# Stores and weight loads in other slots, and two blocks' exponentials taken from PSUM, in a kernel of chunk attention and two feed-forward layers

## Chip, cores and metric

The kernel runs on one core of a Trainium2 chip. The metric is the time of one execution in microseconds (us) on the device, lower is better. The engines are named as the profile names them: PE (TensorE, matmul), PEld (its weight loads), DVE (VectorE), ACT (ScalarE), POOL (GpSimd) and SP (SyncE), whose queue issues every DMA of this kernel.

## What is computed

Attention within chunks of 64 positions, then a gated layer, then a layer with a clipped quadratic activation, each followed by a projection:

```python
# q, k, v: (8 batches, 8 heads, 576 positions, 64), chunks of 64
scores = scale * matmul(q_c, k_c^T); scores -= max(scores)
attn = exp(scores); attn /= sum(attn) + 1e-9
x = matmul(attn, v_c)            # as (4608 tokens, 512)
gate = 1 / (1 + exp(-(x @ w_gate))); val = x @ w_val      # (512, 1536) each
y = (gate * val) @ w_out         # (1536, 512)
h = y @ w_in                     # (512, 2048)
g = where(h >= 1, h, where(h <= -1, 0, (h + 1)**2 / 4))
out = g @ w_out2                 # (2048, 512)
```

The inputs are fp32, except that the weights arrive as 64-bit numbers whose two words the kernel puts together itself ("rounding" below).

## The kernel before

**Blocks and slots.** The 4608 tokens are handled in 9 blocks of 512. The first stage, up to 743.8 us, is a loop over the blocks `b` and over the 12 groups `f` of 128 gate and value columns. Each `(b, f)` has two slots, numbered `24 * b + 2 * f` for the gate projection and one more for the value projection: 216 slots. A projection is 12 matmuls of 128x512 on PE (`pr`, L476 to L478). After the gate projection ACT takes the sigmoid into a tile `sg` (L880, four such tiles in turn), after the value projection DVE multiplies into it (L883), and SP stores it to `gT` in DRAM (`g_store`, L766).

**What lies between the projections.** Everything else of the stage is hung on slots by a table, `at(slot, prio, fn, args)`, and `emit(slot)` writes out what is due, ordered by the slot's fraction, then by `prio`, then by when it was entered. Every engine works its instructions off in the order in which they are written. So the table sets the order on each queue; it sets no time.

**Attention.** The attention of block `b` is spread over slots of block `b - 1`, as four head pairs `p`. Per pair: loads of q and k (`load`, 8 or 16 DMAs, L282) and of v (`v_load`, 4 or 6 DMAs, L297); `t`, transposes on DVE (`qkT`, L307); `s`, the scores on PE into two PSUM banks (`S`, L324); `m`, row maxima on DVE and their subtraction into the SBUF tile `sp` (L334, L338); `e`, the exponential on ACT in place (L344); `n`, the row sums and reciprocals on DVE (L349 to L352); `w`, the multiplication by the reciprocals on POOL (L357); `p`, a transpose on PE (`PT`, L363); `c`, its copy by ACT (L366); `o`, the product with v on PE (`O`, L377); `x` and `l`, the high part by ACT and the low part by DVE (L393, L397), which the projections of the next block read. From block 2 on a pair begins every 6 slots, with `s` in its slot 2, `p` in 6, `c` in 7 and `o` in 8. Block 1 begins a pair every 5 slots. Block 0 has nothing to hide behind: `first_block` writes its four pairs out by hand ahead of the first projection, by the string `ORDER`, where `s` stands for `s`, `m`, `e` in a row, `n` for `n`, `w`, `p` for `p`, `c` and `o` for `o`, `x`, `l`.

**Rounding of weights.** In slots 26 to 186 the weights of the later layers are prepared, one pair of row blocks every 7 slots (`s_prep`): two loads of 512 KB into tiles `raw` (`w_load`, L103 or L107), from 4 slots later on DVE `w_low` (L112), `w_bits` (L118) and `w_join` (L129), ACT `w_scale` (L125), POOL sums (L151 to L154), then four pieces `st` on ACT and POOL (`s_split`, L173 and L174) that SP stores again (`s_spool`, L183). `raw` and `st` share a ring of `pool["nraw"]` tiles, 8 of them.

The later stages (from 743.8 us: three further products) are not touched by the change.

Of the kernel before, what the change touches and what calls it, by code (L numbers as in the profile page):

```python
# [8 lines left out]
F32 = mybir.dt.float32  # L9
# [4 lines left out]
AF = mybir.ActivationFunctionType  # L14
ALU = mybir.AluOpType
AX = mybir.AxisListType
# [13 lines left out]
def kernel(  # L30
# [15 lines left out]
    nc = tc.nc  # L46
    P = 128
# [5 lines left out]
    CH = 64  # L53
    BS = 512
    scale = 1.0 / float(D) ** 0.5
    NB = NT // BS
# [10 lines left out]
    cp = ctx.enter_context(tc.tile_pool(name="cp", bufs=1))  # L67
# [6 lines left out]

    NWT = {"o": 7 * F1 // 4, "i": 7 * F2 // 4, "p": 7 * F2 // 4}
    sw = {kind: dp.tile([n, P, 2, 2, 256], F32, name=f"sw{kind}") for kind, n in NWT.items()}

    def f32(t):
# [118 lines left out]
    def s_prep(kind, k):  # L197

        half_ = (F1 if kind == "o" else F2) // 2
        a, b = (kind, k), (kind, k + half_)  # L200
        return [
            (0, w_load, a), (0, w_load, b), (4, w_low, a), (4, w_bits, a), (5, w_scale, a), (5, w_low, b),
            (5, w_bits, b), (6, w_scale, b), (6, w_join, a), (7, w_join, b), (8, s_sums, kind, k),
            (9, s_split, kind, k, 0), (9, s_split, kind, k, 1), (10, s_split, kind, k, 2),
            (11, s_spool, kind, k, 0), (11, s_spool, kind, k, 1), (11, s_split, kind, k, 3),
            (12, s_spool, kind, k, 2), (13, s_spool, kind, k, 3),
        ]


# [2 lines left out]
    pool = {}  # L212
    X = {}

    def open_pool(key, name, side=None):
        ctx_ = ExitStack()
        pool[key] = ctx_.enter_context(tc.tile_pool(name=name, bufs=1, side=side, reuse_waits="tile"))
        pool[key + "_ctx"] = ctx_

    def close_pool(key):  # L220
        pool[key + "_ctx"].close()
# [12 lines left out]
    NC = BS // P  # L234
# [3 lines left out]
    class Whole:  # L238
# [15 lines left out]
        def load(self, p):  # L254
# [10 lines left out]
            for i, src in enumerate((q, k)):  # L265
                for off, m, bb, s0 in runs(self.b * BS, BS):
                    rows = src[bb, 2 * p:2 * p + 2, s0:s0 + m]
                    part = slice(off // NC, (off + m) // NC)
                    if how == "M":
                        nc.sync.dma_start(  # L270
                            out=t[part, i].rearrange("i h j d -> i h (j d)"),
                            in_=rows.rearrange("h (i j) d -> i h (j d)", j=NC),
                        )
                    elif how == "T":
                        for h in range(2):
                            nc.sync.dma_start(
                                out=t[part, i, :, h], in_=rows[h].rearrange("(i j) d -> i j d", j=NC)
                            )
                    else:
                        for g in range(4):  # L280
                            h, j = divmod(g, 2)
                            nc.sync.dma_start(  # L282
                                out=t[32 * g:32 * g + 32, i, off // 32:(off + m) // 32],
                                in_=rows[h, :, 32 * j:32 * j + 32].rearrange("(t i) r -> i t r", i=32),
                            )
            self.qk[p] = t

        def v_load(self, p):

            self.V[p] = t = self.alloc("vd").rearrange("p i (c e) -> p (i c) e", e=D)  # L290
            half_ = BS // 2
            for off, m, bb, s0 in runs(self.b * BS, BS):
                for swap in range(2):
                    lo, hi = max(off, swap * half_), min(off + m, (swap + 1) * half_)
                    for h in range(2):
                        if lo < hi:
                            nc.sync.dma_start(  # L297
                                out=t[heads[h ^ swap], lo // CH:hi // CH],
                                in_=v[bb, 2 * p + h, s0 + lo - off:s0 + hi - off].rearrange("(c k) d -> k c d", k=CH),
                            )  # L300
# [26 lines left out]
            self.B["s", p] = banks  # L327

        def m(self, p):
            s = self.SP[p][:, 0].rearrange("p (g h k) -> p g h k", h=2, k=CH)  # L330
            m = cp.tile([P, 2, NC], F32, tag="m0", name="m", bufs=2)
            banks = self.B.pop(("s", p))
            for h, b in enumerate(banks):
                nc.vector.tensor_reduce(out=m[:, h], in_=b, axis=AX.X, op=ALU.max)  # L334
            for h, b in enumerate(banks):
                for swap in range(2):
                    gs = slice(swap * NC // 2, (swap + 1) * NC // 2)
                    nc.vector.tensor_tensor(  # L338
                        out=s[:, gs, h ^ swap], in0=b[:, gs],
                        in1=m[:, h, gs].unsqueeze(2).to_broadcast([P, NC // 2, CH]), op=ALU.subtract,  # L340
                    )

        def e(self, p):
            nc.scalar.activation(self.SP[p][:, 0], self.SP[p][:, 0], AF.Exp, scale=scale)  # L344

        def n(self, p):
            s = self.SP[p][:, 0].rearrange("p (g k) -> p g k", k=CH)
            l = cp.tile([P, 2 * NC], F32, tag="l0", name="l", bufs=2)
            nc.vector.tensor_reduce(out=l, in_=s, axis=AX.X, op=ALU.add)  # L349
            nc.vector.tensor_scalar_add(l, l, 1e-9)  # L350
            self.B["r", p] = r = cp.tile([P, 2 * NC], F32, tag="r0", name="r", bufs=2)
            nc.vector.reciprocal(out=r, in_=l)  # L352
# [127 lines left out]
    def proj(key, b, tag):  # L480
        w = W[key]
        o = ps.tile([P, BS], F32, tag=tag, name="pr")
        kts = [slice(kt * P, (kt + 1) * P) for kt in range(KT)]
        three(o, [(w[:, 0, ks], w[:, 1, ks], X[b, kt][:, 0], X[b, kt][:, 1]) for kt, ks in enumerate(kts)])
        return o
# [61 lines left out]
    def run_step(t):  # L547
        for _, _, fn, args in sorted(sched.pop(t, []), key=lambda e: e[:2]):
            fn(*args)
# [203 lines left out]
    NS = 2 * F1  # L753
# [3 lines left out]
    def at(slot, prio, fn, *args):  # L757
        order[0] += 1
        ev.setdefault(int(slot // 1), []).append((slot % 1, prio, order[0], fn, args))

    def emit(slot):
        for _, _, _, fn, args in sorted(ev.pop(slot, []), key=lambda e: e[:3]):
            fn(*args)
# [20 lines left out]
    slot = 26  # L784
    for kind, n in (("o", F1 // 2), ("i", F2 // 2), ("p", F2 // 2)):
        for pair in range(n):
            for dt, fn, *args in s_prep(kind, pair):
                at(slot + dt, 6 + dt / 10, fn, *args)
            slot += 7
    base = NS * (NB - 1)  # L790
    at(base, 8, close_pool, "u")
# [9 lines left out]
    for i in range(FIRST):  # L801
        key, name = ("o", 0, i), ("o", 0, 1, i)
# [52 lines left out]
    with tc.manual_schedule():  # L855
        half = cp.tile([P, 1], F32, name="half")
        nc.vector.memset(half, 0.5)
        minus = cp.tile([P, 1], F32, name="minus")
        nc.vector.memset(minus, -0.5)

        open_pool("pad", "pad", "right")
        pool["pad"].tile([P, 24], F32, name="pad")

        open_pool("pad4", "pad4", "right")
        pool["pad4"].tile([P, 704], F32, name="pad4")
        open_pool("x", "xp", "right")
        open_pool("sg", "sg", "right")
        open_pool("raw", "raw", "right")
        pool["nraw"] = 8
        open_pool("u", "au")  # L870
        first_block()
        for t in range(-6, 0):
            emit(t)
        for b in range(NB):
            for f in range(F1):
                slot = NS * b + 2 * f
                emit(slot)
                go = proj(("g", f), b, f"b{f % 2}")
                sg = pool["sg"].tile([P, BS], F32, tag="sg", name="sg", bufs=4)
                nc.scalar.activation(sg, go, AF.Sigmoid)  # L880
                emit(slot + 1)
                vo = proj(("v", f), b, f"b{2 + f % 2}")
                nc.vector.tensor_tensor(out=sg, in0=vo, in1=sg, op=ALU.mult)  # L883
                at(slot + 2, 7, g_store, b, f, sg)
        emit(NS * NB)
        close_pool("sg")
        assert not ev, ev
        open_pool("r", "rb", "right")
        for t, (fn, *args) in enumerate(steps):
            run_step(t)  # L890
            fn(*args)
        for t in sorted(sched):
            run_step(t)
        for key in ("r", "zb", "pad", "za", "y"):
            close_pool(key)
# [30 lines left out]
```

## Time and profile before

| | |
|---|---|
| median of 3 runs | 1726.3 us (1725.25 to 1729.65) |
| profiled execution | 1722.68 us, of which the span from first to last instruction is 1720.9 |
| PE busy | 1654.2 us, 96% of the span |
| DVE, ACT, POOL busy | 69%, 51%, 48% |
| DMA engines | 57.6% of 16 engines' span, 1505 issues, all on SP's queue |
| mean granted clock of TensorE | 0.984 |

The profiled execution is 3.6 us below the median of the runs; sums below are made against its span and carried over to the median as a difference. A timeline row reads: start, length, engine, line, operation, out<-in and count, and in brackets how long the engine was idle before it and who ended that. For SP a row is the time in which the queue issues the DMAs named, waits between them included; how long the data takes is a matter of other rows.

### The profile page before, as it was taken

To read this page: it belongs to the slowest core of one execution; us is meant where nothing else is said; L and a number is where in the kernel's file an instruction comes from. 1 tells how busy PE (TensorE), PEld (TensorE's weight loads), DVE (VectorE), ACT (ScalarE), POOL (GpSimd) and SP (SyncE) were. 2 spreads that over 40 slices of the span, in tenths; PEclk is the share of its full clock that TensorE was granted. 3 is DMA by queue.
4 is the path that set the end of the run, shared out by engine and by line. 5 is a ranking of instruction groups with operands and counts; after the bars stand their busy time and mean duration, and the time that the engine had idled before them with its cause. 6 is when DMAs were issued, how large, how long until landed. Compare 5 with 4: busy or idle time off the path is not lost.

```text
span 1720.9 us, 30155 instructions
## 1 busy us (share of the span) xinstructions
PE 1654.2 (96%) x10658; PEld 1518.5 (88%) x10658; DVE 1191.2 (69%) x1874; ACT 870.3 (51%) x1632; POOL 834.5 (48%) x755
## 2 busy tenths in 40 slices
PE   5889998998998999999999999999999999999998
PEld 4668886886876888899999999999999999999998
DVE  5875555564554562178777768887887879788877
ACT  4654444554544553145555555555554455545453
POOL 1431433443333442057777754534441476777675
PEclk7989999999999999999999999999999999999999
DMA  7664677776776785824554654233327954463552
GB/s 190 169 161 111 193 220 209 195 211 186 218 211 188 211 269 175 334 95 155 209 166 143 236 207 181 111 141 142 151 109 264 356 194 116 120 182 107 125 139 38
DMA packets 389671, 307.16 MB, mean 178 GB/s; under 512 B 271888, under 2 KB 302608, under 8 KB 389520
## 3 DMA queue, kind: packets, MB, share of 16 engines
q1 hardware_dynamic: 389520, 305.23, 57.6%
q8 instruction: 84, 1.38, 0.3%
q14 instruction: 67, 0.55, 0.1%
HBM read 179.83 MB, written 125.30 MB: 177 GB/s over the span
## 4 chain that ended last, share of the span: by engine, by line
PE 75%; SPq 8%; DVE 6%; DMA 6%; issue 2%; POOL 2%; ACT 1%; DVEq 0%; POOLq 0%; ACTq 0%
PE P L477 17%; PE P L478 17%; PE P L476 17%; PE pr L476 8%; PE pr L477 7%; PE pr L478 7%; SPq L282 5%; DVE z L509 2%; SPq L297 2%; DMA gT<-sg 1%; DMA raw<-in_moe_w_gate_dram 1%; PE O L377 1%; DVE z L520 1%; PE S L324 1%; DMA raw<-in_moe_w_in_dram 1%
## 5 line engine op out<-in xcount | busy, mean ns | idle before, releaser
L520 POOL TENSOR_TENSOR z<-z 128x384 fp32r<-128x384 f32 x305 | 356.4, 1191 | 308.1 <-ACT z L513 305.9
L477 PE MATMUL P<-z,w 128*128 128x384 f32 x1344 | 450.6, 335 | 5.1 <-POOL z L520 3.1
L476 PE MATMUL P<-z,w 128*128 128x384 f32 x1344 | 449.5, 334 | 0.2 <-DVE R L537 0.2
L478 PE MATMUL P<-z,w 128*128 128x384 f32 x1344 | 449.1, 334 | 0.0
L476 PE MATMUL pr<-x,w 128*128 128x512 f32 x864 | 349.0, 404 | 0.0
L477 PE MATMUL pr<-x,w 128*128 128x512 f32 x864 | 341.4, 395 | 0.3 <-DVE x L397 0.3
L478 PE MATMUL pr<-x,w 128*128 128x512 f32 x864 | 341.4, 395 | 0.0
L513 ACT ACTIVATE z<-z 128x384 fp32r<-128x384 f32 x420 | 205.8, 521 | 181.3 <-DVE z L509 106.9
L520 POOL TENSOR_TENSOR op<-in,op 128x384 fp32r<-128x384 f32 x168 | 190.6, 1153 | 148.0 <-ACT op L513 147.1
L477 PEld LDWEIGHTS P<-z,w 128*128 128x128 f32 x1344 | 252.3, 188 | 9.2 <-POOL z L520 6.6
L476 PEld LDWEIGHTS P<-z,w 128*128 128x128 f32 x1344 | 252.3, 188 | 1.1 <-DVE R L537 0.5
L478 PEld LDWEIGHTS P<-z,w 128*128 128x128 f32 x1344 | 252.3, 188 | 0.0
L883 DVE TENSOR_TENSOR sg<-pr,sg 128x512 f32<-128x512 f32 x108 | 74.5, 690 | 221.1 <-PE pr L478 118.1
L478 PEld LDWEIGHTS pr<-x,w 128*128 128x128 f32 x864 | 165.0, 191 | 35.9
L476 PEld LDWEIGHTS pr<-x,w 128*128 128x128 f32 x864 | 165.3, 191 | 35.4
L477 PEld LDWEIGHTS pr<-x,w 128*128 128x128 f32 x864 | 165.4, 191 | 33.5 <-DVE x L397 0.7
L513 ACT ACTIVATE op<-in 128x384 fp32r<-128x384 f32 x252 | 128.5, 523 | 112.8 <-PE P L478 60.1
L880 ACT ACTIVATE sg<-pr 128x512 f32<-128x512 f32 x108 | 64.5, 597 | 221.8 <-PE pr L478 212.0
L509 DVE TENSOR_TENSOR z<-z 128x384 f32<-128x384 f32 x200 | 172.4, 912 | 1.0 <-POOL z L520 0.9
L477 PE MATMUL P<-op,w 128*128 128x384 f32 x504 | 168.5, 334 | 0.1
L478 PE MATMUL P<-op,w 128*128 128x384 f32 x504 | 168.4, 334 | 0.0
L476 PE MATMUL P<-op,w 128*128 128x384 f32 x504 | 168.4, 334 | 0.0
(63 smaller groups left out, 2241.3 us busy)
## 6 DMA issues: line engine op xcount, KB each, us to landing
uT<-ua SPq DMA_DIRECT2D x96, 384.0 KB, 2.4
z<-uT SPq DMA_DIRECT2D x96, 384.0 KB, 4.1
gT<-sg SPq DMA_DIRECT2D x108, 256.0 KB, 4.4
in<-gT SPq DMA_DIRECT2D x72, 256.0 KB, 3.7
raw<-in_moe_w_out_dram SPq DMA_DIRECT2D x28, 512.0 KB, 6.2
w<-swi SPq DMA_DIRECT2D x28, 512.0 KB, 5.6
w<-swp SPq DMA_DIRECT2D x28, 512.0 KB, 6.8
swi<-st SPq DMA_DIRECT2D x24, 512.0 KB, 4.1
```

The costliest lines, as they stand in the source:

```text
L282: nc.sync.dma_start(out=t[32 * g:32 * g + 32, i, off // 32:(off + m) // 32], in_=rows[h, :, 32 * j:32 * j + 32].rearrange("(t i) r -> i t ...
L297: nc.sync.dma_start(out=t[heads[h ^ swap], lo // CH:hi // CH], in_=v[bb, 2 * p + h, s0 + lo - off:s0 + hi - off].rearrange("(c k) d -> k c ...
L324: nc.tensor.matmul(banks[h][heads[c % 2], c // 2], lhsT=t[hs, 0, ts], rhs=t[hs, 1, ts], start=True, stop=True)
L377: nc.tensor.matmul(banks[r][heads[r ^ swap], g_, i], lhsT=self.V[p][rows, c], rhs=self.SP[p][rows, 1, chunks[c]], start=True, stop=True,)
L476: nc.tensor.matmul(o, lhsT=ah, rhs=bh, start=first, stop=False, skip_group_check=open_)
L477: nc.tensor.matmul(o, lhsT=ah, rhs=bl, start=False, stop=False, skip_group_check=open_)
L478: nc.tensor.matmul(o, lhsT=al, rhs=bh, start=False, stop=last, skip_group_check=open_)
L509: (eng or nc.vector).tensor_tensor(out=op_src(p, key), in0=x, in1=y, op=ALU.subtract)
L513: nc.scalar.activation(o[:, 0], op_src(p, key), AF.Copy)
L520: eng.tensor_tensor(out=o[:, 1], in0=op_src(p, key), in1=f32(o[:, 0]), op=ALU.subtract)
L880: nc.scalar.activation(sg, go, AF.Sigmoid)
L883: nc.vector.tensor_tensor(out=sg, in0=vo, in1=sg, op=ALU.mult)
```

## The change

`s_prep` gives every step but the two loads one slot more, and the call enters the table one slot earlier. So the steps stay in the slots they had, and the two `w_load`s of each pair move one slot ahead. The priorities, `6 + dt / 10`, grow by 0.1 for the steps that have one slot more. `g_store` goes from 2 slots behind its projection's to 4. The ring of `raw` and `st` has 10 tiles for 8. For blocks 0 and 1 the scores stay in PSUM: `m_scaled` takes the maxima and multiplies them by `-scale`, and `e_sums` takes 8 exponentials of 128x64 from PSUM with the maximum as bias and the row sum as a second output, so that the subtraction and the row-sum reduction of DVE fall away.

```diff
-            (0, w_load, a), (0, w_load, b), (4, w_low, a), (4, w_bits, a), (5, w_scale, a), (5, w_low, b),
-            (5, w_bits, b), (6, w_scale, b), (6, w_join, a), (7, w_join, b), (8, s_sums, kind, k),
...
+            (0, w_load, a), (0, w_load, b), (5, w_low, a), (5, w_bits, a), (6, w_scale, a), (6, w_low, b),
+            (6, w_bits, b), (7, w_scale, b), (7, w_join, a), (8, w_join, b), (9, s_sums, kind, k),
...
+        def m_scaled(self, p):
+            m = cp.tile([P, 2, NC], F32, tag="m1", name="m", bufs=2)
+            for h, b in enumerate(self.B["s", p]):
+                nc.vector.tensor_reduce(out=m[:, h], in_=b, axis=AX.X, op=ALU.max)
+            nc.vector.tensor_scalar_mul(m, m, -scale)
+            self.B["m", p] = m
+
+        def e_sums(self, p):
...
+            for h, b in enumerate(self.B.pop(("s", p))):
+                for g in range(NC):
+                    r = h ^ (g >= NC // 2)
+                    nc.scalar.activation(
+                        s[:, g, r], b[:, g], AF.Exp, bias=m[:, h, g:g + 1], scale=scale,
+                        accum_out=l[:, g, r:r + 1],
+                    )
+
         def e(self, p):
+            if self.b < 2:
+                return self.e_sums(p)
             nc.scalar.activation(self.SP[p][:, 0], self.SP[p][:, 0], AF.Exp, scale=scale)
...
-                at(slot + dt, 6 + dt / 10, fn, *args)
+                at(slot - 1 + dt, 6 + dt / 10, fn, *args)
...
-        pool["nraw"] = 8
+        pool["nraw"] = 10
...
-                at(slot + 2, 7, g_store, b, f, sg)
-        emit(NS * NB)
+                at(slot + 4, 7, g_store, b, f, sg)
+        for t in range(3):
+            emit(NS * NB + t)
```

PE's order is the same before and after. Three places show what moves on other queues.

ACT in block 0, from pair 2's exponential on (`qkT` is pair 3's, the first `x` pair 0's). Before:

```order
L344 ACTIVATE sp<-sp 128x512
L316 ACTIVATE qkT<-T 128x4x128 x2
L393 ACTIVATE x<-O 64x256 x4
L366 ACTIVATE sp<-PT 128x512
L344 ACTIVATE sp<-sp 128x512
L393 ACTIVATE x<-O 64x256 x4
L366 ACTIVATE sp<-PT 128x512
```

After:

```order
L360 ACTIVATE sp,l<-S,m 128x64 x8
L316 ACTIVATE qkT<-T 128x4x128 x2
L420 ACTIVATE x<-O 64x256 x4
L393 ACTIVATE sp<-PT 128x512
L360 ACTIVATE sp,l<-S,m 128x64 x8
L420 ACTIVATE x<-O 64x256 x4
L393 ACTIVATE sp<-PT 128x512
```

Nothing changes places; one exponential has become eight, with the sums `l` as a second output.

DVE at the same place, from pair 2's maxima to pair 1's low part. Before:

```order
L334 TENSOR_REDUCE m<-S 128x4 x2
L338 TENSOR_TENSOR sp<-S,m 128x2x64 x4
L349 TENSOR_REDUCE l<-sp 128x8
L350 TENSOR_SCALAR l<-l 128x8
L352 RECIPROCAL r<-l 128x8
L397 TENSOR_TENSOR x<-O,x 64x256 x4
L334 TENSOR_REDUCE m<-S 128x4 x2
L338 TENSOR_TENSOR sp<-S,m 128x2x64 x4
L397 TENSOR_TENSOR x<-O,x 64x256 x4
```

After:

```order
L348 TENSOR_REDUCE m<-S 128x4 x2
L349 TENSOR_SCALAR m<-m 128x8
L377 TENSOR_SCALAR l<-l 128x8
L379 RECIPROCAL r<-l 128x8
L424 TENSOR_TENSOR x<-O,x 64x256 x4
L348 TENSOR_REDUCE m<-S 128x4 x2
L349 TENSOR_SCALAR m<-m 128x8
L424 TENSOR_TENSOR x<-O,x 64x256 x4
```

Per pair four subtractions and one reduction are gone and a small multiplication has come.

SP around slot 60 (block 4's first q and k, block 3's last v, the weights of the sixth pair). Before:

```order
L183 DMA swo<-st 128x2x512 x3
L282 DMA qk<-in_q_dram 32x8x32 x8
L282 DMA qk<-in_k_dram 32x8x32 x8
L766 DMA gT_68<-sg 128x512
L183 DMA swo<-st 128x512
L297 DMA vd<-in_v_dram 64x3x64 x2
L297 DMA vd<-in_v_dram 64x64 x2
L297 DMA vd<-in_v_dram 64x4x64 x2
L107 DMA raw<-in_moe_w_out_dram 128x512 x2
L766 DMA gT_68<-sg 128x512 x2
```

After:

```order
L183 DMA swo<-st 128x2x512 x3
L282 DMA qk<-in_q_dram 32x8x32 x8
L282 DMA qk<-in_k_dram 32x8x32 x8
L107 DMA raw<-in_moe_w_out_dram 128x512 x2
L793 DMA gT_68<-sg 128x512
L183 DMA swo<-st 128x512
L297 DMA vd<-in_v_dram 64x3x64 x2
L297 DMA vd<-in_v_dram 64x64 x2
L297 DMA vd<-in_v_dram 64x4x64 x2
L793 DMA gT_68<-sg 128x512 x2
```

The weight loads stand ahead of a store, a spool and six loads of v; the store in each place is that of the product one older than before.

## Rows read from the trace of the kernel before

**Rows 1.** Two stretches: length, busy time of the five engines, granted clock, DMA share, GB/s.

```profile
41.30:130.00 88.70, 74.95 (x529) 58.17 (x526) 72.37 (x137) 54.01 (x86) 34.91 (x26) 0.91 0.62 162
...
254.00:580.00 326.00, 302.80 (x2312) 245.38 (x2305) 176.54 (x375) 155.48 (x260) 123.73 (x128) 0.97 0.71 204
```

**Rows 2.** Timeline of PE: the product steps `O` of slots 56, 62 and 68.

```profile
235.57 0.69 PE L377 MATMUL O<-sp,vd 64*64 64x64 f32 x32
...
253.71 0.69 PE L377 MATMUL O<-sp,vd 64*64 64x64 f32 x32
...
277.94 1.13 PE L377 MATMUL O<-sp,vd 64*64 64x64 f32 x32 [4.98 <-ACT sp L366]
```

**Rows 3.** Timeline of SP's queue: stores of slots 20 to 24 and 26 to 30.

```profile
132.69 7.49 SPq L766 DMA_DIRECT2D gT<-sg  x3
...
154.03 4.28 SPq L766 DMA_DIRECT2D gT<-sg  x3
```

**Rows 4.** What SP waited for from 41 to 640 us (total, times, longest), first row.

```profile
SPq L766 <- DVE sg L883: 20.3, 13, 5.9
```

**Rows 5.** Timeline of SP's queue from 265 to 278 us.

```profile
265.70 0.40 SPq L766 DMA_DIRECT2D gT<-sg  x1
...
266.67 3.89 SPq L297 DMA_DIRECT2D vd<-in_v_dram  x6
270.90 0.81 SPq L107 DMA_DIRECT2D raw<-in_moe_w_out_dram  x2
...
272.75 2.09 SPq L183 DMA_DIRECT2D swo<-st  x2
276.96 0.33 SPq L766 DMA_DIRECT2D gT<-sg  x1
```

**Rows 6.** Timeline of DVE at 275 us: the first conversion of those weights.

```profile
275.06 0.43 DVE L112 TENSOR_SCALAR raw<-raw 128x512 int32<-128x512 uint32 x1 [9.48 <-DMA raw<-in_moe_w_out_dram]
```

**Rows 7.** Timeline of ACT: a sigmoid and the copy behind it; a later sigmoid.

```profile
251.09 0.60 ACT L880 ACTIVATE sg<-pr 128x512 f32<-128x512 f32 x1 [1.77 <-PE pr L478]
251.59 0.59 ACT L366 ACTIVATE sp<-PT 128x512 f32<-128x512 f32 x1
...
507.73 0.60 ACT L880 ACTIVATE sg<-pr 128x512 f32<-128x512 f32 x1 [2.21 <-PE pr L478]
```

**Rows 8.** SP's issue of the store that frees the tile of that later sigmoid.

```profile
504.59 0.37 SPq L766 DMA_DIRECT2D gT<-sg  x1
```

**Rows 9.** DMA issues from 500 to 510 us: count, size, median us to landing.

```profile
gT<-sg SPq DMA_DIRECT2D x2, 256.0 KB, 2.4
```

**Rows 10.** Timeline of ACT in block 0: exponentials of pairs 2 and 3.

```profile
24.52 0.63 ACT L344 ACTIVATE sp<-sp 128x512 f32<-128x512 f32 x1 [2.15 <-DVE sp L338]
...
31.43 0.63 ACT L344 ACTIVATE sp<-sp 128x512 f32<-128x512 f32 x1 [2.67 <-DVE sp L338]
31.97 1.29 ACT L393 ACTIVATE x<-O 64x256 fp32r<-64x256 f32 x4
```

**Rows 11.** Timeline of DVE: pair 2 of block 0; last, pair 0 of block 1.

```profile
22.99 0.70 DVE L334 TENSOR_REDUCE m<-S 128x4 f32<-128x256 f32 x2
23.61 0.87 DVE L338 TENSOR_TENSOR sp<-S,m 128x128 f32<-128x128 f32 x4
25.18 0.69 DVE L349 TENSOR_REDUCE l<-sp 128x8 f32<-128x512 f32 x1 [0.69 <-ACT sp L344]
25.90 0.17 DVE L350 TENSOR_SCALAR l<-l 128x8 f32<-128x8 f32 x1
...
76.55 1.53 DVE L397 TENSOR_TENSOR x<-O,x 64x256 fp32r<-64x256 f32 x4 [0.54 <-ACT x L393]
```

**Rows 12.** ACT groups with a per-partition bias, by shape: busy, mean ns, idle before.

```profile
L668 ACT ACTIVATE ua<-R,half 128x768 f32<-128x768 f32 x48 | 44.7, 932 | 28.8 <-DVE R L537 28.8
L668 ACT ACTIVATE ua<-R,half 128x384 f32<-128x384 f32 x48 | 29.4, 612 | 47.2 <-DVE R L537 47.2
L660 ACT ACTIVATE ua<-P,half 128x384 f32<-128x384 f32 x48 | 27.6, 574 | 10.1 <-PE P L478 10.1
```

More of the change, by code (lines that the diff above doesn't have):

```diff
@@ L201, in s_prep @@
         return [
-            (0, w_load, a), (0, w_load, b), (4, w_low, a), (4, w_bits, a), (5, w_scale, a), (5, w_low, b),
-            (5, w_bits, b), (6, w_scale, b), (6, w_join, a), (7, w_join, b), (8, s_sums, kind, k),
-            (9, s_split, kind, k, 0), (9, s_split, kind, k, 1), (10, s_split, kind, k, 2),
-            (11, s_spool, kind, k, 0), (11, s_spool, kind, k, 1), (11, s_split, kind, k, 3),
-            (12, s_spool, kind, k, 2), (13, s_spool, kind, k, 3),
+            (0, w_load, a), (0, w_load, b), (5, w_low, a), (5, w_bits, a), (6, w_scale, a), (6, w_low, b),
+            (6, w_bits, b), (7, w_scale, b), (7, w_join, a), (8, w_join, b), (9, s_sums, kind, k),
+            (10, s_split, kind, k, 0), (10, s_split, kind, k, 1), (11, s_split, kind, k, 2),
+            (12, s_spool, kind, k, 0), (12, s_spool, kind, k, 1), (12, s_split, kind, k, 3),
+            (13, s_spool, kind, k, 2), (14, s_spool, kind, k, 3),
         ]
@@ L329, in m @@
         def m(self, p):
+            if self.b < 2:
+                return self.m_scaled(p)
             s = self.SP[p][:, 0].rearrange("p (g h k) -> p g h k", h=2, k=CH)
@@ L341, in m @@
                     )
+        def m_scaled(self, p):
[5 more added lines that the diff above has]
+        def e_sums(self, p):
+            s = self.SP[p][:, 0].rearrange("p (g h k) -> p g h k", h=2, k=CH)
+            self.B["l", p] = l = cp.tile([P, NC, 2], F32, tag="l1", name="l", bufs=2)
+            m = self.B.pop(("m", p))
+            for h, b in enumerate(self.B.pop(("s", p))):
[5 more added lines that the diff above has]
+                    )
         def e(self, p):
+            if self.b < 2:
+                return self.e_sums(p)
             nc.scalar.activation(self.SP[p][:, 0], self.SP[p][:, 0], AF.Exp, scale=scale)
         def n(self, p):
-            s = self.SP[p][:, 0].rearrange("p (g k) -> p g k", k=CH)
-            l = cp.tile([P, 2 * NC], F32, tag="l0", name="l", bufs=2)
-            nc.vector.tensor_reduce(out=l, in_=s, axis=AX.X, op=ALU.add)
+            if self.b < 2:
+                l = self.B.pop(("l", p)).rearrange("p g h -> p (g h)")
+            else:
+                s = self.SP[p][:, 0].rearrange("p (g k) -> p g k", k=CH)
+                l = cp.tile([P, 2 * NC], F32, tag="l0", name="l", bufs=2)
+                nc.vector.tensor_reduce(out=l, in_=s, axis=AX.X, op=ALU.add)
             nc.vector.tensor_scalar_add(l, l, 1e-9)
```

## The prediction

> **What bounds the kernel now.** I first read busy time by stretches, since 96% of PE over the whole span says nothing of where time is lost. From 743.8 us on the change touches nothing, and from 130 to 254 PE has no gap. PE loses time in two stretches of the first stage [rows 1]: from 41.3 to 130 us it is busy for 74.95 of 88.70 us at a mean granted clock of 0.91, and from 254 to 580 for 302.80 of 326.00 at 0.97. The second loses 23.2 us of idle time and, at 0.03 of 326, about 10 us of clock. So each of those stops costs more than its idle time.
>
> Next, the timeline of PE in the second stretch. Six slots take 253.71 - 235.57 = 18.1 us where nothing stops, so two slots are 6.0; the next six take 24.2 [rows 2]. The stop of 4.98 us is `O` waiting for ACT's copy. Following it back: ACT's weight scaling stands ahead of that copy, and it waits for DVE, which sat 9.48 us in `w_low` for a weight load [rows 6]. SP issued that load only at 270.90, behind a store, a spool and six loads of v [rows 5].
>
> So why is SP late? Its row of six loads of v takes 3.89 us and ends where the next row begins [rows 5]: the queue is late because it never stops issuing. It waited for a product to store 20.3 us in 13 pieces from 41 to 640 us [rows 4]; two stretches hold nearly half of that: three stores take 7.49 us and three more 4.28, where a store's issue takes 0.40 [rows 3, 5], so 6.3 and 3.1 us are waits, 9.4 together, all by 158 us. After that SP falls behind PE: the store written in slot 60 leaves at 265.70, 12.0 us or four slots of 3.0 after `O` of slot 62 [rows 2, 5]. **PE is held by SP's queue there**, and only the place at which it is felt is a weight load.
>
> **The change, part by part.**
>
> *Stores two slots later, weight loads one slot earlier.* No DMA is added or dropped, so what changes is only what SP does while it waits. The 9.4 us of waits before 158 us were for products; a store that is two slots older asks for a product 6.0 us older, so SP can run ahead by 6.0 of the 9.4 us. All later loads leave up to 6.0 us earlier, and the weight loads of the worst pair also pass the v loads, 270.90 - 265.70 = 5.2 us [rows 5]. Together 11.2, more than the 9.48 us that DVE waited for them [rows 6]. The other two stops of this kind have the same order (6 and 7 slots meet every 42), so the weight loads stop being what comes last.
>
> What is late next is the tile `sg`. There are four, so the sigmoid 8 slots on needs the store landed. In the order the store is 6.0 us later, on the clock SP is up to 6.0 us ahead: the stores leave about when they do now, while PE, no longer stopped, comes earlier and meets them. The gain is therefore no more than the slack that the tightest store has now. That one leaves at 504.59 [rows 8], lands some 2.4 us later [rows 9] at 507.0, and its tile's sigmoid starts at 507.73 [rows 7]: 0.7 us. To this comes what ACT can be late without PE noticing. At the same place of another pair the sigmoid starts at 251.09, its copy ends at 252.18, `O` starts at 253.71 [rows 2, 7]: 1.5 us. And to this the wait before the store at 276.96 (272.75 + 2.09 = 274.84, so 2.1 us [rows 5]), which an older product no longer causes and which shifts all that SP issues after it. Sum: 0.7 + 1.5 + 2.1 = **4.3 us gained**. Bounds: 8 us, if stores at the next tightest places have 3 to 4 us more slack; on the other side a loss of 3.8, if SP's lead doesn't come about: 6.0 - 0.7 - 1.5.
>
> *Ten tiles in the ring, steps in the same slots.* The conversions keep their slots and only a priority grows, and nothing stands between; I cost it at nothing. The two more tiles take waits of ACT for spools away, which ACT's idle time covers (155 of 326 us busy [rows 1]); the cost of that cover being gone is inside the bounds above.
>
> One rule of the Trainium skill speaks against this whole part. The trace has SP issue without a stop, at 0.65 us for a load of v [rows 5]. The Trainium skill, "DMA: Bandwidth & Descriptors", section "Issuing engines are not separate DMA queues", says that the time a sequencer takes to initiate a DMA is usually small beside the DMA itself. By that the place in SP's order would be worth nothing; this case's rows disagree, since here SP's issuing is what a weight load waits behind.
>
> *Eight exponentials in place of one.* An ACTIVATE with a per-partition bias takes (932 - 612) / 384 = 0.83 ns per column, and from PSUM 574 ns at 384 [rows 12], so 574 - 320 x 0.83 = 308 ns at 64 columns. Four pieces of 64x256 follow each other in 1.29 us [rows 10], so back to back little is saved. Eight take 2.0 us when they overlap as those do, if the row sum costs nothing. No row shows a row sum on ACT; as a bound from above I charge another instruction of that size without columns, 308 - 53 = 255 ns, less overlap, say 0.21 each: 3.7 us. Between 2.0 and 3.7 I take 2.9, the middle, since the nearest row (a bias, no sum) is the lower end and something is to be added. One exponential now takes 0.63 [rows 10]: ACT +2.3 us per pair. DVE loses 0.87 of subtractions and 0.69 of row sums and gains a multiplication of 0.17 [rows 11]: -1.4.
>
> *Block 0* has nothing to hide behind. Between maxima and the end of the exponentials lies -0.87 + 0.17 + 2.3 = +1.6 us per pair. Pair 2's maxima start at 22.99 [rows 11], kept by DVE's sums of pair 1; those lose 0.69 but wait for pair 1's longer exponentials, and the scores of pair 2 wait for the same banks, so I let this start stand. Pair 3's maxima stand behind the low part of pair 0 on DVE, that behind `x` on ACT, that behind pair 2's exponentials; and `x` of pair 1 stands right behind pair 3's (31.43, 31.97 [rows 10]). So two pairs count in full, and with rounding **+3.1 us** until the first projection. At 2.0 us for eight, pair 2 starts 1 us earlier: +0.4; at 3.7, it starts later too: +5.5.
>
> *Block 1.* DVE is busy for 72.37 of 88.70 us and PE waits for it [rows 1]; less DVE work is the point. But the chain passes through ACT: `l` on DVE waits 0.54 us for `x` on ACT [rows 11], and ACT's `x` stands behind the exponential. Per pair DVE gives 0.70 ahead of the exponentials and 0.69 behind, ACT takes 2.3, and an earlier start of some 0.8 makes up the rest, so about nothing per pair; in the last pair DVE waits for a weight load, which covers it. I take **-0.3**, with -2.5 if eight take 2.0 us and +2.0 if 3.7. The scores' banks are held some 1.5 us longer, covered by a pair's five slots.
>
> Sum: 3.1 - 0.3 - 4.3 = **-1.5 us**, a span of 1719.4 for 1720.9. The profiled execution is 3.6 us below the median of the runs; the same difference from 1726.3 gives 1724.8.
>
> **Rivals.**
>
> *The tile `sg` takes over (slower).* Place: ACT's sigmoid in the slot before a copy, every sixth slot. If SP is held by its own issuing before 130 us and can't use the waits, or PE's later start eats the lead, the stores land 6.0 us later with 2.2 of slack: +3.8 instead of -4.3. Then 3.1 - 0.3 + 3.8 = +6.6: 1732.9. It decides once the lead is under 3.8 us. For it: SP issues nearly without stop from 41 us. Against: 9.4 us of waits are in the rows.
>
> *Cheap row sums (faster).* Eight exponentials at 2.0 us: 0.4 - 2.5 - 4.3 = -6.4: 1719.9. For it: eight instructions of 308 ns are all that a row shows. Against: a second output that costs nothing.
>
> *The order on SP is worth nothing.* The change then doesn't do what it is written for: 3.1 - 0.3 = +2.8, 1729.1, as the rule above would have it. Against it are the rows on SP; the trace bears the rule out only where SP does wait.
>
> **How the numbers follow.** A difference under 0.3%, 5.2 us, is about what a measurement of this kernel can't tell from none. My forecast, 0.36, lies within; the order worth nothing, 0.10, too. Slower 0.27: the `sg` rival, with the upper end of block 0 beside it. Faster 0.27: cheap sums, or the 8 us of slack. The range goes from about -8 (cheap sums with some more slack) to +7 (the `sg` rival): 1718 to 1733.5.
>
> **What would show it.** Right: `O` of slot 68 without a stop for weights, the wait in `w_low` there gone; SP ahead by some 6 us at the loads of slot 30; ACT waiting for `gT<-sg` where PE stops; the first projection some 3 us later. Wrong: eight exponentials outside 2.0 to 3.7 us; the first projection no later; or the stretch from 254 to 580 us shorter by more than 8 us, which would mean that stores land sooner than I read.

## The result and the profile after

The changed kernel takes 1736.85 us (median of 5 runs, 1733.21 to 1740.18) against 1726.3 (5 runs, 1723.06 to 1729.65): ratio 1.0066, 95% interval 1.0048 to 1.0083, so 8 to 14 us slower. That lies above the whole forecast range. The profiled execution of after is its longest (1740.18), that of before lies 3.6 us under its median, so the two traces differ by 17 us, 7 more than the medians. Below, places are read from traces and sizes from times, or from several traces.

The start of a slot's first matmul divides the span. Four starts on PE, of slots 0, 24 and 168 and of what is called the last stage here, the last two products, whose matmuls are `P<-z`. In before:

```profile
41.34 0.79 PE L476 MATMUL pr<-x,w 128*128 128x512 f32 x1
...
139.24 0.48 PE L476 MATMUL pr<-x,w 128*128 128x512 f32 x1
...
606.83 0.48 PE L476 MATMUL pr<-x,w 128*128 128x512 f32 x1
...
1006.29 0.33 PE L476 MATMUL P<-z,w 128*128 128x384 f32 x1
```

In after:

```profile
43.64 0.50 PE L503 MATMUL pr<-x,w 128*128 128x512 f32 x1
...
144.34 0.48 PE L503 MATMUL pr<-x,w 128*128 128x512 f32 x1
...
617.81 0.48 PE L503 MATMUL pr<-x,w 128*128 128x512 f32 x1
...
1017.67 0.34 PE L503 MATMUL P<-z,w 128*128 128x384 f32 x1
```

Block 0 has cost 2.3 us, slots 0 to 24 (block 1's attention) 2.8, slots 24 to 168 5.9, the untouched middle 0.4. From 1017.67 to the end of the span (1738.1) are 720.4 us, where before has 714.6: 5.8 more, in a stage that no line of the diff names.

The two stretches of [rows 1] in after (length, busy time of the five engines, granted clock, DMA share, GB/s):

```profile
41.30:130.00 88.70, 71.69 (x512) 55.44 (x512) 68.32 (x120) 57.19 (x141) 32.61 (x24) 0.90 0.61 159
254.00:580.00 326.00, 303.16 (x2262) 245.73 (x2260) 177.23 (x373) 153.32 (x259) 124.01 (x128) 0.98 0.71 201
```

DVE is relieved in block 1 (68.32 for 72.37) and yet PE does less there (71.69 for 74.95), which is in part the later start: slot 0 begins 2.3 us later in the same stretch. In the second stretch PE is as busy as before. Here are waits from 254 to 580 us (total, times, longest), of before:

```profile
DVE raw L112 <- DMA raw<-in_moe_w_out_dram: 29.7, 6, 9.5
...
DVE raw L112 <- DMA raw<-in_moe_w_in_dram: 24.2, 8, 10.1
...
ACT sg L880 <- DMA gT<-sg: 3.1, 1, 3.1
...
PE O L377 <- ACT sp L366: 14.1, 3, 5.6
```

and of after:

```profile
ACT sg L907 <- DMA gT<-sg: 68.4, 13, 8.7
...
ACT L907 <- DMA gT<-sg: 12.8, 3, 6.2
...
DVE raw L112 <- DMA raw<-in_moe_w_in_dram: 10.4, 6, 3.5
...
PE O L404 <- ACT sp L393: 20.4, 10, 4.8
```

`w_low` waited 53.9 us for weight loads in before and 14.7 in after (10.4 and 4.3); the sigmoid waited 3.1 us for the store that frees its tile and now waits 81.2. At `O` the weight loads no longer come last; `sg` does, at 16 sigmoids, and PE waits there 20.4 us in ten pieces where it waited 14.1 in three. One of the sigmoids on ACT, with the copy that `O` needs behind it, and two of PE's stops at `O`, at slots 68 and 74 (compare [rows 2]):

```profile
439.15 0.60 ACT L907 ACTIVATE sg<-pr 128x512 f32<-128x512 f32 x1 [8.04 <-DMA gT<-sg]
439.65 0.59 ACT L393 ACTIVATE sp<-PT 128x512 f32<-128x512 f32 x1
```

```profile
278.67 0.69 PE L404 MATMUL O<-sp,vd 64*64 64x64 f32 x32 [1.14 <-ACT sp L393]
300.25 0.97 PE L404 MATMUL O<-sp,vd 64*64 64x64 f32 x32 [2.85 <-ACT sp L393]
```

The stop of 4.98 at slot 68 is 1.14; a new one stands at slot 74. SP's stretches of [rows 3] now read

```profile
130.95 8.03 SPq L793 DMA_DIRECT2D gT<-sg  x3
...
153.30 4.67 SPq L793 DMA_DIRECT2D gT<-sg  x3
```

12.7 us for 11.8: the products asked for are older, but block 1 makes them later. So on the clock SP is no earlier, but beside PE it is. The loads of slot 30 leave at, before and after:

```profile
162.47 4.04 SPq L282 DMA_DIRECT2D qk<-in_q_dram  x8
```

```profile
161.99 5.11 SPq L282 DMA_DIRECT2D qk<-in_q_dram  x8
```

From the start of slot 24 that is 23.2 us before and 17.7 after. In the traces of this document it is 23.2 to 24.0 in the ten with the stores in their old slots and 17.6 to 17.9 in the eight with the stores two slots later. The lead of some 6 us that the prediction names came about, as a lead on PE.

### The profile page after: what moved, and what is told of

Same layout as the page of the kernel before. It is cut to its first block, busy times and chain, and to the rows that moved or that the text cites. A ratio compares the mean times of both kernels' runs of the same rounds, so it can differ in the third digit from the quotient of the medians.

```text
span 1738.1 us, 30182 instructions
## 1 busy us (share of the span) xinstructions
PE 1665.3 (96%) x10658; PEld 1530.3 (88%) x10658; DVE 1182.0 (68%) x1842; ACT 881.9 (51%) x1752; POOL 834.4 (48%) x755
## 4 chain that ended last, share of the span: by engine, by line
PE 77%; SPq 8%; DMA 6%; DVE 4%; issue 2%; ACT 1%; POOL 1%; ACTq 0%; DVEq 0%; POOLq 0%
PE P L504 18%; PE P L505 18%; PE P L503 18%; PE pr L503 8%; PE pr L504 7%; PE pr L505 7%; SPq L282 5%; DMA gT<-sg 3%; SPq L297 2%; DMA raw<-in_moe_w_gate_dram 1%; DVE z L536 1%; PE O L404 1%; PE S L324 1%; DMA vd<-in_v_dram 1%; DMA raw<-in_moe_w_val_dram 1%
## 5 line engine op out<-in xcount | busy, mean ns | idle before, releaser
L536 DVE TENSOR_TENSOR z<-z 128x384 f32<-128x384 f32 x200 | 168.5, 892 | 1.0 <-POOL z L547 0.9
```

Of the source, the lines that this page charges most:

```text
L536: (eng or nc.vector).tensor_tensor(out=op_src(p, key), in0=x, in1=y, op=ALU.subtract)
```

## The experiments

Ratios are to runs of the kernel before beside them, with 95% intervals. The medians of those runs differ (1725.8 to 1728.2 us), so small differences between experiments are better read from the ratios. Line numbers are those of each kernel.

**One part at a time.** The exponentials alone (`m_scaled` and `e_sums` for `self.b < 2`, nothing else):

> The kernel before with the exponentials of blocks 0 and 1 from PSUM alone (stores, weight loads and ring as before). Theory A (from about 160 to 590 us SP's issuing holds PE; SP's rows of before and after lie within a few us of each other on the clock): slot 24 starts 5.1 us later, as in the changed kernel, but PE then waits that much less for weight loads, so slot 168 is only 0 to 2 us later: 1726 to 1729 us. Rival B (what the first two blocks lose stays lost): +5.1 us, 1731.4.

1737.49 us, 1.0060 (1.0042 to 1.0079): the whole loss, and neither number. Theory A's giving back did not happen, and B's 5.1 us are too few.

```diff
-                at(slot + 2, 7, g_store, b, f, sg)
+                at(slot + 4, 7, g_store, b, f, sg)
```

> The kernel before with the stores of the products two slots later, nothing else. Theory A (the tile sg ties PE to SP: with a store in slot 4 behind its projection only 4 slots are left to land it before the sigmoid that takes the tile, where there were 6): ACT waits for gT<-sg about every 6 slots from slot 60 on, the three stops for weights stay in part, slot 24 is where it was, slot 168 is 4 to 10 us later: 1730 to 1737 us. Rival B (the stores cost nothing, the loss is the first two blocks'): 1726 within 2.

1722.70 us, 0.9975 (0.9961 to 0.9989). ACT's waits for `gT<-sg` came as expected (51.6 us from 254 to 580), the loss did not: the kernel is some 4 us faster, which neither theory had.

```diff
-                at(slot + dt, 6 + dt / 10, fn, *args)
+                at(slot - 1 + dt, 6 + dt / 10, fn, *args)
...
-        pool["nraw"] = 8
+        pool["nraw"] = 10
```

(with the steps other than the loads one slot more, as in the change)

> The kernel before with the weight loads one slot earlier and ten tiles in the ring, stores two slots behind their projection and exponentials as before. Theory A: the three stops in w_low at slots 68, 110 and 152 go, as in the changed kernel, and the store with 0.7 us of slack takes over late: slot 168 is 3 to 8 us earlier, 1718 to 1723 us. Rival B (SP's place in the order is worth nothing, PE is held by SP's total of issues): 1726 within 2.

1720.61 us, 0.9966 (0.9952 to 0.9980), as theory A had it. From 254 to 580 us PE waits 0.5 us at `O` for the copy, where before had 14.1, and the sigmoids wait 7.5 us for stores (6.8 and 0.7):

```profile
ACT sg L907 <- DMA gT<-sg: 6.8, 5, 3.6
...
PE O L404 <- ACT sp L393: 0.5, 1, 0.5
```

It is the stores' two slots, and not the loads' one, that make `sg` come last. The two more tiles of the ring were not tried apart from the loads. Both slot edits together, with the old exponentials:

> The changed kernel without its exponentials: stores two slots later, weight loads one slot earlier, ten tiles in the ring; blocks 0 and 1 as before. Theory A: slot 24 as before, then stops for gT<-sg that eat the gain: by slot 168 PE is nearly as late as in the changed kernel, 7 to 11 us, 1733 to 1737 us. Rival B (costs add): the changed kernel less 5.1 us, 1731.7.

1722.32 us, 0.9975 (0.9960 to 0.9989). Neither theory: the slot edits are a gain of about 4 us, the single gains don't add up, and the loss comes with the exponentials.

**Which exponentials.** Block 0 alone (`self.b < 1`) and block 1 alone (`self.b == 1`):

> The kernel before with the exponentials from PSUM in block 0 alone. Theory C (the eight exponentials of 2.4 us lengthen the chain ACT, DVE, POOL, PE once per pair, in block 0 by some 2.5 us in all and in block 1 by 1 to 1.5 us a pair; what is late by slot 24 stays late, since SP waits for the products of block 1): the first projection starts at about 43.5 us, slot 24 is 2 to 3.5 us later than without: 1729 to 1731 us. Rival D (the late first projection alone puts the loads of block 1 out of step and costs most of the 10 us): 1734 or more.

> The kernel before with the exponentials from PSUM in block 1 alone. Theory C: the first projection as before, slot 24 some 4 to 7 us later than without, DVE's waits for ACT's high part (x) up from some 5 to 8 us between 43 and 142 us: 1731 to 1735 us. Rival D: 1729 or less.

1735.08 us, 1.0039 (1.0022 to 1.0056), and 1736.21, 1.0045 (1.0026 to 1.0065). Each alone costs two thirds to three quarters of both, so something seems to be paid once by either. In the two traces slot 168 is 3.4 and 4.9 us later than in the first trace of before, the end of the span 9.7 and 12.9: the rest is in the last stage. Next, the exponentials without the sums, which DVE takes as before:

```diff
-                        accum_out=l[:, g, r:r + 1],
```

> Exponentials of blocks 0 and 1 from PSUM with the maximum as bias, but without the accumulated row sums: DVE reduces the rows as in the kernel before. Tells whether the accumulator reads or the eight pieces cost. Eight take about 1.8 us in place of 2.4 (ACT 0.6 shorter per pair), DVE gets its 0.69 us back per pair. If the chain runs through ACT alone, 3 to 5 us below the kernel with accumulated sums (1737.5), 1733 to 1735; if what ACT gives DVE takes, 1737 to 1739; if the pieces cost nothing without the reads, back to 1727.

1730.71 us, 1.0023 (1.0007 to 1.0039). The expectation took this for the price of the sums, and it isn't: this kernel also lacks the tile `l1`, and its last stage is not slow (710.0 us from its first start to its last). Against the kernel with sums and an unmoved `z` (1.0031, below) the sums are not shown to cost anything: the intervals overlap.

**Where tiles lie.** The new tiles `m1` and `l1` take 128 bytes of each partition ahead of tiles `z`, the operand that the last stage streams: the first tile of that name moves from 116608 to 116736, and the others on its side with it. First the move without the change, then the change without the move:

```diff
-            self.B["r", p] = r = cp.tile([P, 2 * NC], F32, tag="r0", name="r", bufs=2)
+            self.B["r", p] = r = cp.tile([P, 4 * NC + 8], F32, tag="r0", name="r", bufs=2)[:, :2 * NC]
```

> The kernel before with the two tiles of the reciprocals made 64 bytes longer each, so that every tile behind them in SBUF lies 128 bytes further, as in the changed kernel (tile z at 116736 for 116608); no instruction differs. Theory E (the last stage, from about 1006 us on, is slower by some 6 us in each kernel with the new tile l1, since z lies elsewhere): its matmuls go from 173.3 to 175.3 ns apart, the stage from 708.5 to 714.5 us: 1732 to 1735 us. Rival F (the accumulator reads on ACT do it): the stage stays at 708.5, 1727 within 2.

```diff
-            m = cp.tile([P, 2, NC], F32, tag="m1", name="m", bufs=2)
+            m = cp.tile([P, 2, NC], F32, tag="m0", name="m", bufs=2)
...
-            self.B["l", p] = l = cp.tile([P, NC, 2], F32, tag="l1", name="l", bufs=2)
+            self.B["l", p] = l = cp.tile([P, NC, 2], F32, tag="l0", name="l", bufs=2)
```

> The changed kernel with its maxima and sums in the tiles that the other blocks use (m0 and l0), so that z lies where it lay before; the instructions are the changed kernel's. Theory E: the last stage is back at 708.5 us and the whole at 1729 to 1732 us. Rival F: 1736 to 1738.

The kernel before with the move alone: 1733.08 us, 1.0036 (1.0021 to 1.0051). The change without it: 1731.96, 1.0030 (1.0019 to 1.0041), for 1.0066. The last stage's matmuls on the page (busy, mean ns), moved and unmoved:

```profile
L476 PE MATMUL P<-z,w 128*128 128x384 f32 x1344 | 454.0, 338 | 0.0
```

```profile
L503 PE MATMUL P<-z,w 128*128 128x384 f32 x1344 | 449.2, 334 | 0.0
```

Theory E holds in both directions, with the same instructions: about half of the loss is an address. Both kernels with one block alone have the move too; that is what either pays.

One trace shows by itself that it is the streamed tile. Of the 22 tiles `z` that the last stage streams, 14 (pool `za`) lie behind the new ones and move; 8 (pool `zb`) are taken from the other end of SBUF and stay. In the first of the two products a matmul of after that streams a moved tile is followed by the next 176.0 ns later, one that streams an unmoved tile 173.4 ns (means of 1344 and 671 pitches under 200 ns); in before it is 173.4 and 173.3. The other four traces with the move give 176.0 and 173.4 too. The exponentials without the move:

> The kernel before with the exponentials of blocks 0 and 1 from PSUM alone, their small tiles shared so that z lies where it lay. Theory E: 6 us under the kernel with tiles of its own (1737.5), so 1730 to 1732.5: the exponentials themselves cost 3 to 5.5 us. Rival F: 1736 to 1738.

1732.78 us, 1.0031 (1.0019 to 1.0042), 5.4 us (3.3 to 7.2).

**Block 1.** Second pair of block 1 in that kernel: ACT from its first exponential on (`O` of the pair before ended at 76.05), and DVE:

```profile
76.09 1.28 ACT L360 ACT_TABLE_LOAD   x1
77.38 0.31 ACT L360 ACTIVATE sp<-S,m 128x64 f32<-128x64 f32 x1
77.59 0.19 ACT L360 ACTIVATION_READ_ACCUMULATOR sp<-S,m 128x1 f32 x1
77.69 0.30 ACT L360 ACTIVATE sp<-S,m 128x64 f32<-128x64 f32 x1
...
80.81 1.31 ACT L420 ACTIVATE x<-O 64x256 fp32r<-64x256 f32 x4
```

```profile
82.16 1.53 DVE L424 TENSOR_TENSOR x<-O,x 64x256 fp32r<-64x256 f32 x4 [2.35 <-ACT x L420]
83.70 0.17 DVE L377 TENSOR_SCALAR l<-l 128x8 f32<-128x8 f32 x1
```

ACT's `x` has its input at 76.05 and begins at 80.81, behind a table load, the exponentials and two steps for weights (1.1 us); the table load stands in before too. DVE waits for `x`, and the reciprocals stand behind that. So `x` was written ahead of those exponentials:

```diff
-    later_block(1, [5 * p for p in range(KT)], (0, 1, 1.5, 2, 3, 3, 5, 5.5, 7, 7.5, 8))
+    later_block(1, [5 * p for p in range(KT)], (0, 1, 1.5, 2, 3, 3, 5, 5.5, 7, 7, 8))
```

> The kernel with only the exponentials changed and z where it lay (1732.8), and in block 1 ACT's high part x of a pair written ahead of the next pair's exponentials, where it stood two steps behind them; DVE's order is the same. Theory G (block 1 loses because x stands behind eight exponentials on ACT and DVE waits for it): DVE's waits for x between 43 and 142 us fall from 8 to 11 us to under 4, slots 0 to 24 take 95 to 98 us in place of 100.6: 1727 to 1730 us. Rival H (the pair's own chain maxima, exponentials, reciprocals, transpose is what is longer): slots 0 to 24 stay at 100 to 101, 1732 within 1.5.

1728.60 us, 1.0021 (1.0009 to 1.0033). DVE's waits for `x` from 43 to 142 us, in the kernel without and with the step:

```profile
DVE x L424 <- ACT x L420: 11.9, 5, 3.9
```

```profile
DVE x L424 <- ACT x L420: 1.9, 1, 1.9
```

Slots 0 to 24 take 97.1 us for 100.6, inside theory G's range, as is the time. The two ratios' intervals overlap, so it is the waits, more than the time, that show what the step does.

**The tile `sg`.** A fifth tile, with the slot edits and the old exponentials, then with the whole change and `z` unmoved:

```diff
-                sg = pool["sg"].tile([P, BS], F32, tag="sg", name="sg", bufs=4)
+                sg = pool["sg"].tile([P, BS], F32, tag="sg", name="sg", bufs=5)
```

> Stores two slots later, weight loads one slot earlier, ten tiles in the ring, exponentials as before, and five tiles sg in place of four. Theory (PE is tied to SP by the ring of sg: 83 us of waits for gT<-sg from 240 to 600 us with four tiles, 3 in the kernel before): a fifth tile gives two slots back, the waits for gT<-sg fall under 25 us, PE's stops with them: 1714 to 1719 us. Rival (PE is held by the sum of what SP issues): as with four tiles, 1722 within 2.

> The changed kernel with z where it lay before and five tiles sg. If the exponentials' delay stays through the first stage, it is above the kernel with five tiles and the old exponentials (1715.5) by the 5 to 8 us that they cost by slot 24: 1720 to 1724 us. If SP, which then has more time ahead of PE, gives the delay back: 1715.5 to 1718.

1715.49 us, 0.9927 (0.9901 to 0.9952), 8 to 17 us faster than before and the fastest here; and 1724.21, 0.9987 (0.9978 to 0.9996). Waits of the sigmoid from 254 to 580 us, with four tiles and with five (old exponentials):

```profile
ACT sg L907 <- DMA gT<-sg: 80.7, 14, 8.3
...
ACT L907 <- DMA gT<-sg: 15.3, 5, 6.0
```

```profile
ACT sg L907 <- DMA gT<-sg: 5.1, 5, 3.0
```

The two kernels with five tiles differ by 8.7 us, about what the exponentials lose by slot 24 (9.6 between these two traces): SP doesn't give it back. With `x` ahead as well:

> The kernel with the slot changes, five tiles sg and the old exponentials (1715.5), with the same step of x in block 1. Theory G, with one exponential of 0.63 us ahead of x: a gain of 0 to 2 us, 1713.5 to 1715.5. Rival H: no change, or a loss of up to 2 us since ACT then waits for the product O.

1717.07 us, 0.9945 (0.9931 to 0.9960): no gain, outside theory G's range and as rival H allows. DVE's waits for `x` fall from 5.1 to 2.1 us and slots 0 to 24 take 95.0 us for 93.7: with one exponential ahead of `x` the step is worth nothing.

**Chance.** One more execution each of the kernel before and of the slot edits:

> The kernel before once more, for a second trace: if slots 0 to 24 take 93 to 98 us by chance from execution to execution, this one lies anywhere there; if the stores' slots matter in that stretch, it lies at 97 to 98.5 as in the two traces so far. Slots 24 to 168: 471 to 473 us.

> The kernel with the slot changes alone once more, for a second trace: if the stores' slots matter from slot 0 to 24, that stretch is at 93 to 94.5 us again; if it is chance, anywhere from 93 to 98. Slots 24 to 168: 471 to 473.5 us.

1724.85 and 1724.52 us. Slots 0 to 24 took 94.0 and 97.1, for 97.9 and 93.3 in the first traces, so that stretch varies by some 4 us between executions of one kernel, whatever the stores' slots. By trace, each the difference of two starts, the last stage's from its first matmul to its last (us):

| | slot 0 at | slots 0 to 24 | slots 24 to 168 | last stage |
|---|---|---|---|---|
| before, three traces (one moved) | 41.3, 39.6, 40.0 | 97.9, 98.4, 94.0 | 467.6, 471.6, 473.8 | 708.5, 716.2 moved, 710.0 |
| slot edits, two traces | 42.5, 40.4 | 93.3, 97.1 | 471.5, 472.1 | 708.3, 707.8 |
| exponentials, moved and not | 43.7, 42.5 | 100.9, 100.6 | 473.0, 471.5 | 717.4, 707.8 |
| the change, moved and not | 43.6, 43.0 | 100.7, 100.7 | 473.5, 473.2 | 714.6, 707.8 |
| five tiles, old exponentials and new | 40.7, 42.5 | 93.7, 101.6 | 465.4, 465.3 | 708.6, 708.0 |
| `x` ahead, four tiles and new exponentials | 43.0 | 97.1 | 475.9 | 707.8 |
| `x` ahead, five tiles and old exponentials | 40.3 | 95.0 | 461.3 | 710.4 |
| exponentials in block 0, in block 1 (both moved), without sums | 42.9, 39.5, 41.3 | 94.4, 100.2, 100.2 | 472.9, 472.1, 472.3 | 714.7, 716.1, 710.0 |
| stores alone, loads alone | 40.5, 39.7 | 93.8, 96.1 | 470.0, 466.6 | 708.3, 709.3 |

## Why the prediction was wrong

**"From 743.8 us on the change touches nothing": the step that failed first.** No instruction changes there, but an operand's place does. The move of `z` cost 6.9 us alone (1733.08 less 1726.19) and 4.9 inside the change (1736.85 less 1731.96), where the prediction put the later stages at nothing. No rival had it. Without it the change is at 1731.96, inside the range and slower than before.

**Block 0, forecast +3.1: right.** Slot 0 starts 2.3 us later in the two first traces, 2.6 over all of them (means of 43.0 in seven with the new exponentials there and sums, 42.5 to 43.7, and 40.4 in ten without, 39.5 to 42.5). Eight exponentials took 2.5 us, between the bounds; the middle, 2.9, was a little high.

**Block 1, forecast -0.3: wrong.** Slots 0 to 24 take 100.2 to 101.6 us in seven traces with the new exponentials in block 1 and `x` in its old place, mean 100.7, and 93.3 to 98.4 in nine without and with `x` in its old place, mean 95.4: +5.3, beyond the upper bound of 2.0. The step that failed is "about nothing per pair": I set ACT's longer piece against DVE's savings as if they shared one budget. The row that speaks against it was quoted, `l` waiting 0.54 us for `x` [rows 11]: `x` stands behind the exponentials, so their length goes to that wait, which is 6.1 us in before and 11.3 in after between 43 and 142 us, and what DVE saves doesn't shorten the stretch. Putting `x` ahead took 3.5 us of the 5.3 back, in one trace. The rest is open, and so is why the kernel without sums loses as much (100.2), though its eight exponentials take 1.75 us for 2.48 and its waits for `x` are 8.3. And by time the exponentials cost 5.4 us (3.3 to 7.2), less than 2.6 and 5.3 together; where the difference comes back the traces don't show.

**Order on SP, forecast -4.3: the mechanism right, the size not.** The lead came, the waits in `w_low` went and `sg` came last, as written. The step that failed is the size: the slack of the tightest store, 0.7 + 1.5 + 2.1, was worked out as a limit ("no more than the slack that the tightest store has now") and then taken as the gain. In after 16 sigmoids wait 81.2 us for stores, PE's waits for the copy at `O` go from 14.1 to 20.4 us, and slots 24 to 168 take as long as before: the four traces with both slot edits (471.5 to 473.5) stand among those of before. That is the place of the first rival, but neither its condition, since the lead is there, nor its price of +3.8. In the change the edits give 0.8 us (1732.78 less 1731.96; ratios 1.0031 and 1.0030), which can't be told from nothing. With the old exponentials they give 4.3 by time, the number forecast, but the traces don't show it in the stretch that it was worked out for, nor in which other; so the agreement bears nothing out, and this stays open. That a fifth tile brings 6 to 8 us in slots 24 to 168, with either exponentials, shows that `sg` held PE there.

**The rule weighed in the prediction.** The order on SP is worth something here with the old exponentials (0.9975, and 0.9927 with five tiles). The Trainium skill, "DMA: Bandwidth & Descriptors", section "Issuing engines are not separate DMA queues", calls the time to initiate a DMA usually small relative to the DMA itself. For one DMA the trace agrees: a load of v takes 0.65 us to issue [rows 5] and 2.3 to 4.4 from issue to landing (medians by size, from 41 to 640 us in before). But these times add up on one queue, so the conclusion drawn from the rule, that the order is worth nothing, doesn't hold with the old exponentials; with the new ones no run shows the order to be worth anything until a fifth tile is there (1.0031 for the exponentials, 0.9987 with the edits and the tile).

So the sum, +3.1 - 0.3 - 4.3, should have read +2.6, +5.3, 0 to -4 and, for the moved operand, +5 to +7: 9 to 15. Measured: 8 to 14.

## What to carry to other kernels

When an engine's step gets longer, look for what stands behind it on that engine and who waits for that: time saved on another engine doesn't pay for it, and putting the waited-for step ahead may. When transfers are delayed on purpose, deepen the ring that they release, or the wait only changes its name. And a new small tile moves every tile behind it: let it share a tag, and compare the stages that the diff doesn't touch.

## What the runs showed of the hardware

The matmuls `P<-z` start 173 to 174 ns apart with `z` unmoved and, in after, where the streamed tile has moved by 128 bytes, in a pattern of five:

```
before: 173 173 174 173 173 174 173 173 174 173
after:  182 176 173 174 175 182 176 173 174 175
```

Over the 4032 of the last stage this makes 714.6 to 717.4 us (five traces) for 707.8 to 710.4 (twelve). Moved by 64 bytes (the kernel without sums) one trace has 710.0. The granted clock was 1.00 in the stage in both; why the place matters no run here shows. And an exponential of 128x64 with a row sum is two instructions on ACT, 0.30 to 0.35 us and a read of 0.19 to 0.25, at a pitch of 0.29 us; eight take 2.48 us, and without the sum 1.75.
